# Layer 2 by kind of product in both layers' first slots, and w1's second half and w2 requested behind the gathered rows

## The chip, the cores and the metric

One of the eight cores of a Trainium2 chip runs the whole program. The metric is the device time of one execution in microseconds. TensorE does the matrix products, VectorE, ScalarE and GpSimd the elementwise work; SyncE (SP) mostly issues DMA requests, and GpSimd issues the indexed ones (gathers and scatters of rows).

## The reference, cut to what matters

An attention with a decaying state over 4 sequences of 768 tokens (8 heads of 64) gives 3072 rows of 512 numbers. Two mixture-of-experts layers follow, each with 8 experts; a row goes to one expert, the one with the largest logit:

```python
logits = x @ w_gate + modality_bias[modality_id]      # layer 1; layer 2 without the bias
e_idx = np.argmax(logits, axis=1)
for e in range(E):
    mask = e_idx == e
    h = np.maximum(x[mask] @ w1[e], 0.0)              # 512 -> 1024
    out[mask] = gate_w[mask, None] * (h @ w2[e])      # 1024 -> 512
```

Layer 2 skips rows whose `x @ w_skip` is not positive and adds its result to x.

## The kernel before, in words

**Precision.** Every product of the experts is done as three: each float32 factor is split into a high part (a cast to the matmul's format, `high`, `high_w2` on ScalarE) and a low part (the rest, a subtraction, `low`, `low_w2` on VectorE), and high x high, high x low and low x high are summed in PSUM. The tiles are `xth`/`xtl` (the rows, transposed), `w1h`/`w1l`, `hh`/`hl` (the hidden values after ReLU) and `w2h`/`w2l`; `raw1` and `raw2` hold the weights as loaded.

**Stages.** The attention runs over 24 units i (6 chunks of 128 tokens x 4 sequences). Each loads keys, queries and values, does its products, writes its row tile to `xs1` (`stage_x`), and each chunk's four tiles are routed: logits (`route_1`, copied to `lgt`), a transpose of them on TensorE and the bias (`route_2`), arg max and running sums `rs` on VectorE (`route_3`), the rank within the expert as two small products and the scatter of (row, gate) to a table `tab` (`route_4`, `route_5`). Then come the experts: the sorted rows are worked off in slots of 256 rows (two blocks of 128). A slot gathers its rows by the table (`load_ix`, `gather_x`), transposes them (`trans_x`), does `layer1` over eight blocks f of 128 hidden columns, two to a PSUM bank, and `layer2` over eight blocks c of the hidden dimension for either row block j. Layer 2 has the same slots over the rows of layer 1.

**The first slots.** `first1` begins before the last chunk is routed: its expert is chosen from earlier counts, its rows are gathered in unit 21, and in `layer1` the functions in `steps` and `mids` do the rest of the routing between the blocks f. The tables of later slots (`table`) are made on VectorE meanwhile, in three parts. `first2` is the same for layer 2. All others go through `slot`.

**Order.** Instructions run on each engine in the order in which the Python code issues them; semaphores are added where tiles depend on each other. SP's queue is in order too: a request that waits holds up all behind it. `behind(first, got)` makes a request wait for a gather's landing.

**Lines that the prediction uses** (numbers of the kernel before, which the profile has): L413 stores a row tile, L580 requests w1 by halves, L298 requests w2, L165 gathers; L304/L309 and L319/L322 split w1 and w2; L366 transposes gathered rows, L369/L370 cast them to `xth` and subtract to `xtl`; L548/L556 are attention products; L389 copies the logits to `lgt`, L392 transposes them; L133 are the running sums, L137/L138 the ranking products; L744 is layer 1's product, L751/L754 make `hh` and `hl`; L794, L795 and L796 are layer 2's three kinds of product, L806/L809 its result.

Of the kernel before, what the change touches and what calls it, by code (L numbers as in the profile page):

```python
# [35 lines left out]
def body(ctx: ExitStack, tc: tile.TileContext, qkv, cpk, w1, w2, wgr, out, dbg=None):  # L36
# [251 lines left out]
    def f32(ap):  # L288
        return ap.bitcast(F32)
# [12 lines left out]
    def high(n, cs):  # L302
        for c in cs:
            nc.scalar.copy(out=w1h[c][:, n * D:n * D + D], in_=raw1[:, c, n * D:n * D + D])  # L304
# [16 lines left out]
    def low_w2(c, eng=nc.vector):  # L321
        eng.tensor_tensor(out=w2l[c], in0=raw2[:, 2 * c:2 * c + 2], in1=f32(w2h[c]), op=ALU.subtract)  # L322
# [34 lines left out]
    def behind(first, got):  # L357
        for g in got:
            tc.add_manual_dep(first.ins, g.ins.name, mybir.DependencyInfo(mybir.DependencyClass.Sync, mybir.DependencyReason.DATA),
                              reason="the rows first")  # L360
# [59 lines left out]
    with ExitStack() as actx:  # L420
# [164 lines left out]
        for i in range(N):  # L585
# [13 lines left out]
            if i == N - 2:  # L599
                high(1, (0, 1))  # L600
# [7 lines left out]
            if i == 19:  # L608
                load_ix(0, 0, nc.sync.value_load(eb[0:1, 0, 1:2], min_val=0, max_val=E * TP - T))
                ld_w1_half(e0, 1)  # L610
            if i == N - 2:
                behind(ld_w2(e0), got0)
# [32 lines left out]
            if i == N - 2:  # L645
                low(1, (0, 1))
# [141 lines left out]
    def layer2(which, kk, j, hooks={}, cs=range(8)):  # L788
# [10 lines left out]
        if 7 not in cs:  # L799
            return  # L800
# [20 lines left out]
    def first1():  # L821
        tb = table(0)

        def last_x():
            high(1, (2, 3))
            low(1, (2, 3))
            stage_x(NC * B - 1, ptr[0])
            route_1()
            high_w2(0)
            low_w2(0, nc.gpsimd)  # L830
# [10 lines left out]
        def then():  # L841
            low_w2(1)
            next(tb)

        layer1(0, {0: last_x, 2: lambda: high_w2(1), 3: then, 5: lambda: split_w2([2]), 7: lambda: split_w2([3])},
               mids={1: mid, 3: late}, lead=True)
        next(tb)
# [10 lines left out]
        layer2(0, 0, 0)  # L858
        fl = flag(0, 1)
        layer2(0, 0, 1, {5: lambda: trans_x(0, 1, ptr), 6: lambda: split_next(0, 1, fl)})  # L860
        return fl, is_full(ei[0][0:1, 3 * KT + 1:3 * KT + 2])

    def first2():
# [3 lines left out]
        layer1(0, {0: la, 3: lambda: rb(pcnt[1]), 4: lambda: next(tb), 5: lambda: split_w2([1]),  # L867
               6: lambda: split_w2([2]), 7: lambda: split_w2([3])}, mids={1: rk}, lead=True)
# [11 lines left out]
        layer2(1, 0, 0)  # L880
        next(tb)
        fl = flag(1, 1)
        layer2(1, 0, 1, {5: lambda: trans_x(1, 1, ptr), 6: lambda: split_next(1, 1, fl)})

# [178 lines left out]
```

## Time and profile before

| | |
|---|---|
| median of 3 runs | 684.38 us (683.06 to 685.27) |
| the profiled execution | 685.24 us |
| its span | 683.3 us, of which matmuls in flight 659.0 us |
| granted TensorE clock | 0.996 of full speed |
| attention, to the first product of layer 1 | about 0 to 125 us |
| layer 1's first slot | 125 to 152 us |
| layer 2's first slot | 449.8 to 476 us |

A row of the timeline has the start, the length, the engine and line, the operation, what it writes and reads, and in brackets how long the engine stood idle before it and what released it. The ends of matmuls are modelled, and they overlap, so distances between starts tell more than lengths. Names of tiles stand without their numbers, so that `bank` is any PSUM bank and `xt` any row tile.

### The profile page before, as it was taken

To read this page: it belongs to the slowest core of one execution; us is meant where nothing else is said; L and a number is where in the kernel's file an instruction comes from. 1 tells how busy PE (TensorE), PEld (TensorE's weight loads), DVE (VectorE), ACT (ScalarE), POOL (GpSimd) and SP (SyncE) were. 2 spreads that over 40 slices of the span, in tenths; PEclk is the share of its full clock that TensorE was granted. 3 is DMA by queue.
4 is the path that set the end of the run, shared out by engine and by line. 5 is a ranking of instruction groups with operands and counts; after the bars stand their busy time and mean duration, and the time that the engine had idled before them with its cause. 6 is when DMAs were issued, how large, how long until landed. Compare 5 with 4: busy or idle time off the path is not lost. (4 is left out here: it accounts for less than half of the span.)

```text
span 683.3 us, 16287 instructions
## 1 busy us (share of the span) xinstructions
PE 659.0 (96%) x5388; PEld 587.0 (86%) x5388; DVE 437.0 (64%) x1147; ACT 258.2 (38%) x452; POOL 226.4 (33%) x288
## 2 busy tenths in 40 slices
PE   6999999899999999999999999999999999999993
PEld 5889988789988988889889988897998899888892
DVE  6656577684877916878778327868227575758650
ACT  2434435432122225832122227432225644566520
POOL 4356556461332331244322323323121112113321
PEclk9999999999999999999999999999999999999998
DMA  9768777739512232884211211633716658657500
GB/s 287 230 205 221 224 206 226 224 93 383 193 61 78 80 126 88 289 291 168 74 39 54 95 57 45 226 121 91 263 63 196 214 178 281 201 193 262 198 5 29
DMA packets 60653, 112.07 MB, mean 164 GB/s; under 512 B 18672, under 2 KB 18800, under 8 KB 60384
## 3 DMA queue, kind: packets, MB, share of 16 engines
q1 hardware_dynamic: 48544, 89.01, 39.7%
q0 software_dynamic: 9744, 20.47, 8.8%
q8 instruction: 62, 1.02, 0.7%
q10 hardware_dynamic: 2224, 0.93, 0.6%
q14 instruction: 79, 0.65, 0.3%
HBM read 86.44 MB, written 30.06 MB: 170 GB/s over the span
## 5 line engine op out<-in xcount | busy, mean ns | idle before, releaser
L744 PE MATMUL bank<-xth,w1h 128*128 128x256 f32 x672 | 188.4, 281 | 1.1 <-ACT xth L369 0.3
L744 PE MATMUL bank<-xth,w1l 128*128 128x256 f32 x672 | 187.0, 279 | 0.0
L744 PE MATMUL bank<-xtl,w1h 128*128 128x256 f32 x672 | 186.0, 278 | 0.1
L794 PE MATMUL bank<-w2h,hh 128*128 128x512 f32 x360 | 144.6, 402 | 0.0
L796 PE MATMUL bank<-w2h,hl 128*128 128x512 f32 x360 | 141.5, 393 | 0.3 <-DVE hl L776 0.3
L795 PE MATMUL bank<-w2l,hh 128*128 128x512 f32 x360 | 140.8, 391 | 0.9 <-DVE w2l L322 0.8
L744 PEld LDWEIGHTS bank<-xth,w1h 128*128 128x128 f32 x672 | 126.4, 188 | 3.4 <-issue 1.1
L744 PEld LDWEIGHTS bank<-xtl,w1h 128*128 128x128 f32 x672 | 126.1, 188 | 1.4 <-DVEq L816 0.4
L744 PEld LDWEIGHTS bank<-xth,w1l 128*128 128x128 f32 x672 | 126.4, 188 | 0.9 <-DVE w1l L316 0.7
L751 ACT ACTIVATE hh<-bank 128x512 fp32r<-128x512 f32 x84 | 50.3, 599 | 182.7 <-PE bank L744 141.8
L161 POOL DMA_INDIRECT out_dram<-x2r,it x43 | 51.2, 1190 | 191.6 <-DVE x2r L809 102.6
L754 DVE SCALAR_TENSOR_TENSOR hl<-bank,hh 128x512 fp32r<-128x512 f32 (+1 forms) x100 | 58.2, 601 | 84.2 <-ACT hh L751 78.4
L697 DVE CUSTOM_DVE_ANT_0 xtl<-x2r,wgb 128x512 fp32r<-128x512 f32 x108 | 74.3, 692 | 14.0 <-issue 8.7
L796 PEld LDWEIGHTS bank<-w2h,hl 128*128 128x128 f32 x360 | 67.6, 188 | 15.9 <-DVE hl L776 0.8
L795 PEld LDWEIGHTS bank<-w2l,hh 128*128 128x128 f32 x360 | 67.7, 188 | 15.7 <-DVE w2l L322 2.3
L161 POOL DMA_INDIRECT tab<-pk,rows x28 | 33.0, 1180 | 138.8 <-issue 92.1
L794 PEld LDWEIGHTS bank<-w2h,hh 128*128 128x128 f32 x360 | 67.7, 188 | 12.7
L165 POOL DMA_INDIRECT xg<-xs,it x54 | 58.4, 1081 | 27.7 <-issue 16.7
L322 DVE TENSOR_TENSOR w2l<-raw,w2h 128x1024 fp32r<-128x1024 f32 x47 | 54.7, 1219 | 4.4 <-ACT w2h L319 3.7
L319 ACT CAST w2h<-raw 128x1024 fp32r<-128x1024 f32 x48 | 49.3, 1050 | 20.4 <-issue 12.0
L806 ACT ACTIVATE x2r<-bank,it 128x512 f32<-128x512 f32 x26 | 17.9, 688 | 97.3 <-PE bank L796 76.8
L316 DVE TENSOR_TENSOR w1l<-raw,w1h 128x512 fp32r<-128x512 f32 x88 | 53.9, 684 | 0.6 <-ACT w1h L315 0.3
(207 smaller groups left out, 834.6 us busy)
## 6 DMA issues: line engine op xcount, KB each, us to landing
raw<-in_w_dram SPq DMA_DIRECT2D x96, 512.0 KB
kq<-in_qkv_dram SPq DMA_DIRECT2D x48, 256.0 KB
xs<-x2r SPq DMA_DIRECT2D x28, 256.0 KB
v<-in_qkv_dram SPq DMA_DIRECT2D x24, 256.0 KB
xs<-xr SPq DMA_DIRECT2D x24, 256.0 KB
xs<-xgm SPq DMA_DIRECT2D x7, 512.0 KB
wgb<-in_wgr_dram SPq DMA_DIRECT2D x1, 2304.0 KB
xg<-xs,it POOLq DMA_INDIRECT x54
```

The source lines that it names most:

```text
L161: nc.gpsimd.indirect_dma_start(out=dst, out_offset=bass.IndirectOffsetOnAxis(ap=idx, axis=0), in_=rows, in_offset=None, bounds_check=dst.s ...
L165: return nc.gpsimd.indirect_dma_start(out=rows, out_offset=None, in_=src, in_offset=bass.IndirectOffsetOnAxis(ap=idx, axis=0), bounds_chec ...
L316: nc.vector.tensor_tensor(out=w1l[c][:, s], in0=raw1[:, c, s], in1=f32(w1h[c][:, s]), op=ALU.subtract)
L319: nc.scalar.copy(out=w2h[c], in_=raw2[:, 2 * c:2 * c + 2])
L322: eng.tensor_tensor(out=w2l[c], in0=raw2[:, 2 * c:2 * c + 2], in1=f32(w2h[c]), op=ALU.subtract)
L697: nc.vector.tensor_tensor_reduce(out=xtl[kk % 2][:, :, j * P:(j + 1) * P], in0=x2r[kk % 2][j].rearrange("p (c t) -> p c t", t=P), in1=wgb[ ...
L744: nc.tensor.matmul(o, w[c][:, fs], x[:, c, :], start=(n == 0), stop=(n == 11))
L751: nc.scalar.activation(out=a, in_=pt, func=AF.Relu)
L754: nc.vector.scalar_tensor_tensor(out=b[:, q_], in0=pt[:, q_], scalar=0.0, in1=f32(a[:, q_]), op0=ALU.max, op1=ALU.subtract)
L794: nc.tensor.matmul(p2[j], a, w2h[g][:, i], start=(n == 0), stop=False)
L795: nc.tensor.matmul(p2[j], a, w2l[g][:, i], start=False, stop=False)
L796: nc.tensor.matmul(p2[j], b, w2h[g][:, i], start=False, stop=(n == 7))
```

## The change

Requests: w1's second half leaves unit 19, goes to unit 22 and waits for the first slot's gather (`behind`); w2 leaves unit 22 and goes to unit 23, without a wait of its own. Splits of w1's second half, two pieces of which were done in unit 22, are all done in `last_x`, behind the first block of layer 1. Splits of w2 in the first slots: the high parts are cast between the blocks of layer 1 as before, though at other places, and all low parts are subtracted behind layer 1, on VectorE, where one of four in `first1` was GpSimd's. Products of layer 2 in the first slots: `layer2_wide` does all high x high products of both row blocks, then low x high, then high x low, instead of the three kinds in turn for one block c after the other. The transposes of slot 1's rows follow 46 of the 48 products (before: 42). In `first2` the ranking products keep their place on TensorE, but the rest of the ranking goes ahead of the second ReLU; the last part of the table goes ahead of layer 2's products.

```diff
-    def low_w2(c, eng=nc.vector):
-        eng.tensor_tensor(out=w2l[c], in0=raw2[:, 2 * c:2 * c + 2], in1=f32(w2h[c]), op=ALU.subtract)
+    def low_w2(c):
+        nc.vector.tensor_tensor(out=w2l[c], in0=raw2[:, 2 * c:2 * c + 2], in1=f32(w2h[c]), op=ALU.subtract)
...
-            if i == N - 2:
-                high(1, (0, 1))
...
             if i == 19:
                 load_ix(0, 0, nc.sync.value_load(eb[0:1, 0, 1:2], min_val=0, max_val=E * TP - T))
-                ld_w1_half(e0, 1)
             if i == N - 2:
-                behind(ld_w2(e0), got0)
+                behind(ld_w1_half(e0, 1), got0)
+            if i == N - 1:
+                ld_w2(e0)
...
-            if i == N - 2:
-                low(1, (0, 1))
...
+    def layer2_wide(which, hooks):
+        n = 0
+        for kind in range(3):
+            for j in range(2):
+                js = slice(j * P, (j + 1) * P)
+                for c in range(8):
+                    x = (hh, hl, hh)[kind][c // 4][:, c % 4, js]
+                    w = (w2h, w2h, w2l)[kind][c // 2][:, c % 2]
+                    nc.tensor.matmul(p2[j], x, w, start=(kind == 0 and c == 0), stop=(kind == 2 and c == 7))
+                    if n in hooks:
+                        hooks[n]()
+                    n += 1
+                if kind == 2:
+                    finish(which, 0, j)
...
         def last_x():
-            high(1, (2, 3))
-            low(1, (2, 3))
+            high(1, range(4))
+            low(1, range(4))
             stage_x(NC * B - 1, ptr[0])
             route_1()
-            high_w2(0)
-            low_w2(0, nc.gpsimd)
...
         def then():
-            low_w2(1)
+            high_w2(1)
             next(tb)
-        layer1(0, {0: last_x, 2: lambda: high_w2(1), 3: then, 5: lambda: split_w2([2]), 7: lambda: split_w2([3])},
+        layer1(0, {0: last_x, 2: lambda: high_w2(0), 3: then, 5: lambda: high_w2(2), 6: lambda: high_w2(3)},
                mids={1: mid, 3: late}, lead=True)
+        for c in range(4):
+            low_w2(c)
...
-        layer2(0, 0, 0)
         fl = flag(0, 1)
-        layer2(0, 0, 1, {5: lambda: trans_x(0, 1, ptr), 6: lambda: split_next(0, 1, fl)})
+        layer2_wide(0, {45: lambda: trans_x(0, 1, ptr), 46: lambda: split_next(0, 1, fl)})
...
-        layer1(0, {0: la, 3: lambda: rb(pcnt[1]), 4: lambda: next(tb), 5: lambda: split_w2([1]),
-               6: lambda: split_w2([2]), 7: lambda: split_w2([3])}, mids={1: rk}, lead=True)
+        layer1(0, {0: la, 4: lambda: next(tb), 5: lambda: high_w2(1), 6: lambda: high_w2(2), 7: lambda: high_w2(3)},
+               mids={1: rk, 3: lambda: rb(pcnt[1])}, lead=True)
+        for c in range(1, 4):
+            low_w2(c)
...
-        layer2(1, 0, 0)
         next(tb)
         fl = flag(1, 1)
-        layer2(1, 0, 1, {5: lambda: trans_x(1, 1, ptr), 6: lambda: split_next(1, 1, fl)})
+        layer2_wide(1, {45: lambda: trans_x(1, 1, ptr), 46: lambda: split_next(1, 1, fl)})
```

SP's queue from the index load of the first slot on, before. `raw_136` is w1 as loaded, `raw_137` w2; `xr` are row tiles on their way to `xs`.

```order
L351 DMA it_158<-tab_61 128x2x4
L580 ISA
L580 DMA raw_136<-in_w_dram 128x2x512
...
L413 DMA xs_60<-xr_186 128x512
L438 DMA v<-in_qkv_dram 128x512
L413 DMA xs_60<-xr_187 128x512
L413 DMA xs_60<-xr_185 128x512
L298 ISA
L298 DMA raw_137<-in_w_dram 128x2x512
```

The same stretch now:

```order
L413 DMA xs_60<-xr_186 128x512
L438 DMA v<-in_qkv_dram 128x512
L413 DMA xs_60<-xr_187 128x512
L413 DMA xs_60<-xr_185 128x512
L580 ISA
L580 DMA raw_136<-in_w_dram 128x2x512
...
L413 DMA xs_60<-xr_186 128x512
L298 ISA
L298 DMA raw_137<-in_w_dram 128x2x512
```

w1's two requests (one is shown) stand behind three stores and the last load of values, and w2's four behind one more store.

ScalarE from the last but one row tile on, before. `w1h_138` to `w1h_141` are the four pieces of w1's high part, here of its second half; `xt_191` is the last unit's output.

```order
L304 CAST w1h_138<-raw_136 128x512
L304 CAST w1h_139<-raw_136 128x512
L412 COPY xr_186<-bank_199 128x512
L369 CAST xth_164<-bank_197 128x4x128
L369 CAST xth_164<-bank_200 128x4x128
L558 COPY xt_191<-bank_198 128x512
L304 CAST w1h_140<-raw_136 128x512
L304 CAST w1h_141<-raw_136 128x512
L412 COPY xr_187<-bank_196 128x512
L389 COPY lgt<-pmi 128x128
L319 CAST w2h_146<-raw_137 128x1024
```

And now:

```order
L412 COPY xr_186<-bank_199 128x512
L369 CAST xth_164<-bank_197 128x4x128
L369 CAST xth_164<-bank_200 128x4x128
L558 COPY xt_191<-bank_198 128x512
L304 CAST w1h_138<-raw_136 128x512
L304 CAST w1h_139<-raw_136 128x512
L304 CAST w1h_140<-raw_136 128x512
L304 CAST w1h_141<-raw_136 128x512
L412 COPY xr_187<-bank_196 128x512
L389 COPY lgt<-pmi 128x128
L748 ACTIVATE hh_1855<-bank_195 128x512
```

All four casts of w1's second half stand directly ahead of the copy of the last row tile and of `lgt`.

TensorE's second layer in the first slot of layer 1, before. `bank_200` and `bank_201` are the sums of the two row blocks; `w2h_146` to `w2h_149` and `w2l_150` to `w2l_153` the pieces of w2's high and low part.

```order
L794 MATMUL bank_200<-w2h_146,hh_1859 128x512
L795 MATMUL bank_200<-w2l_150,hh_1859 128x512
L796 MATMUL bank_200<-w2h_146,hl_1861 128x512
L794 MATMUL bank_200<-w2h_146,hh_1859 128x512
L795 MATMUL bank_200<-w2l_150,hh_1859 128x512
L796 MATMUL bank_200<-w2h_146,hl_1861 128x512
L794 MATMUL bank_200<-w2h_147,hh_1859 128x512
```

And now, its first group and the first rows of its last:

```order
L807 MATMUL bank_200<-w2h_146,hh_1855 128x512 x2
L807 MATMUL bank_200<-w2h_147,hh_1855 128x512 x2
L807 MATMUL bank_200<-w2h_148,hh_1856 128x512 x2
L807 MATMUL bank_200<-w2h_149,hh_1856 128x512 x2
L807 MATMUL bank_201<-w2h_146,hh_1855 128x512 x2
...
L807 MATMUL bank_200<-w2l_150,hh_1855 128x512 x2
L807 MATMUL bank_200<-w2l_151,hh_1855 128x512 x2
```

The first low part of w2 was read by the 2nd product and is now read by the 33rd; the last high part was read by the 19th and is now read by the 7th.

## Rows read from the trace of the kernel before

**Rows 1.** The page: busy time of the engines; one costly group.

```profile
PE 659.0 (96%) x5388; PEld 587.0 (86%) x5388; DVE 437.0 (64%) x1147; ACT 258.2 (38%) x452; POOL 226.4 (33%) x288
...
L322 DVE TENSOR_TENSOR w2l<-raw,w2h 128x1024 fp32r<-128x1024 f32 x47 | 54.7, 1219 | 4.4 <-ACT w2h L319 3.7
```

**Rows 2.** Timeline of TensorE where attention ends: start, length, operation, [idle before].

```profile
120.10 1.06 PE L548 MATMUL bank<-qs,sd 128*128 128x128 f32 x8
121.94 0.66 PE L366 MATMUL bank<-ident,xg 128*128 128x128 f32 x4 [0.78 <-DMA xg<-xs,it]
...
123.95 1.09 PE L556 MATMUL bank<-P,v 128*64 128x128 f32 x16
...
129.56 0.27 PE L392 MATMUL pmi<-ident,lgt 128*128 128x128 f32 x1
...
132.50 0.19 PE L137 MATMUL pmi<-oh,tri 128*128 128x32 bf16 x1
133.93 0.18 PE L138 MATMUL pmi<-rs,ones 128*128 128x32 bf16 x1 [1.24 <-DVE rs L133]
```

**Rows 3.** Timeline of TensorE, layer 2's products in layer 1's first slot.

```profile
139.88 0.40 PE L794 MATMUL bank<-w2h,hh 128*128 128x512 f32 x1
...
144.17 0.39 PE L794 MATMUL bank<-w2h,hh 128*128 128x512 f32 x1
144.64 0.50 PE L795 MATMUL bank<-w2l,hh 128*128 128x512 f32 x1
...
150.02 1.03 PE L366 MATMUL bank<-ident,xg 128*128 128x128 f32 x8
...
152.62 0.39 PE L744 MATMUL bank<-xtl,w1h 128*128 128x256 f32 x1
```

**Rows 4.** Timelines of VectorE and GpSimd: running sums, and a split of w2.

```profile
115.49 0.76 DVE L133 TENSOR_TENSOR rs<-rs,oh 128x8 bf16<-128x8 bf16 x4
...
131.21 2.86 DVE L133 TENSOR_TENSOR rs<-rs,oh 128x8 bf16<-128x8 bf16 x4
...
131.08 2.38 POOL L322 TENSOR_TENSOR w2l<-raw,w2h 128x1024 fp32r<-128x1024 f32 x1 [4.83 <-ACT w2h L319]
```

**Rows 5.** Timeline of GpSimd: second gathers of the first slot and of slot 1.

```profile
116.61 1.00 POOL L165 DMA_INDIRECT xg<-xs,it  x1 [0.31 <-issue]
...
146.68 1.15 POOL L165 DMA_INDIRECT xg<-xs,it  x1 [0.31 <-issue]
```

**Rows 6.** Timelines of SP's requests for weights and of ScalarE's first cast of w2.

```profile
103.02 1.00 SPq L580 DMA_DIRECT2D raw<-in_w_dram  x2
...
112.49 1.86 SPq L580 DMA_DIRECT2D raw<-in_w_dram  x2
...
123.47 5.22 SPq L298 DMA_DIRECT2D raw<-in_w_dram  x4
...
129.95 1.05 ACT L319 CAST w2h<-raw 128x1024 fp32r<-128x1024 f32 x1 [1.51 <-DMA raw<-in_w_dram]
```

**Rows 7.** Two stretches: length, engines' busy shares, clock, DMA share, GB/s (last).

```profile
103.00:107.60 4.60, 4.30 (x62) 3.51 (x64) 2.61 (x6) 2.28 (x5) 3.98 (x5) 1.00 0.78 233
...
112.50:118.40 5.90, 5.90 (x71) 5.19 (x70) 5.52 (x20) 2.91 (x6) 3.35 (x3) 1.00 0.63 173
```

**Rows 8.** Timeline of ScalarE: `lgt`, and the last ReLU of either first slot.

```profile
128.18 0.27 ACT L389 COPY lgt<-pmi 128x128 f32<-128x128 f32 x1 [0.41 <-PE pmi L387]
...
141.76 0.60 ACT L751 ACTIVATE hh<-bank 128x512 fp32r<-128x512 f32 x1 [2.97 <-remote]
...
462.64 0.60 ACT L751 ACTIVATE hh<-bank 128x512 fp32r<-128x512 f32 x1 [0.52 <-PE bank L744]
```

**Rows 9.** Timeline of TensorE, layer 2's products in layer 2's first slot.

```profile
462.20 0.40 PE L794 MATMUL bank<-w2h,hh 128*128 128x512 f32 x1
...
473.07 0.60 PE L366 MATMUL bank<-ident,xg 128*128 128x128 f32 x4
474.19 0.66 PE L366 MATMUL bank<-ident,xg 128*128 128x128 f32 x4 [0.52 <-DMA xg<-xs,it]
```

More of the change, by code (lines that the diff above doesn't have):

```diff
@@ L798, in layer2, with finish @@
                 hooks[n]()
-        if 7 not in cs:
-            return
+        if 7 in cs:
+            finish(which, kk, j)
+    def layer2_wide(which, hooks):
[12 more added lines that the diff above has]
+                    finish(which, 0, j)
+    def finish(which, kk, j):
         g = XG(which, kk)[j]
```

## The prediction

> **What bounds the kernel now.** I read the page's busy line first: TensorE has matmuls in flight for 659.0 of 683.3 us [rows 1]. So time can only come out of places where the matmul engine stands still, and the change touches two such places: the first slot of either layer. I then read TensorE's timeline over the first slot of layer 1 (120 to 153 us) and of layer 2 (450 to 476 us), and asked at each gap which engine or transfer ended it. What counts are distances between starts, since the listed ends are modelled.
>
> There are four gaps. (a) The last attention products start at 120.10 and the transposes of the first expert rows at 121.94, released by the gather's landing; the next attention products start at 123.95 [rows 2]. (b) The second ranking product starts 1.43 us after the first, 133.93 against 132.50, released by VectorE's running sums [rows 2]. There the sums need 2.86 us for four tiny additions that took 0.76 us one unit earlier, and the first of them starts 0.13 us after GpSimd began its split of w2's first low part (2.38 us) [rows 4]. (c) In the second layer's products one waits for w2's low part: 144.64 after 144.17, where the pace is (144.17 - 139.88)/18 = 0.238 us [rows 3]. (d) In layer 2's first slot the same wait costs more: 42 products lie between 462.20 and 473.07; at 0.234 us they need 9.83, so 1.04 us is waiting. The last four transposes there wait another 0.52 us for a gather [rows 9].
>
> **The change part by part.** All sums are made against the profiled execution, 685.24 us (683.3 of span, 1.9 around it). It is the slowest of the runs shown; the median is 684.38, and I subtract the difference from that.
>
> *The rows' gather first.* w1's second half (two requests, 1 MB) leaves the place behind unit 19 and now waits for the gather, with w2's four requests behind it. On SP's queue it moves past three stores and one load, which start earlier, and the gather no longer shares the DMA engines with it. The nearest undisturbed gather: the second one issued at 146.68 was in place when TensorE began its transposes at 150.02 without a wait [rows 3, 5], at most 3.34 us. The gather here was issued at 116.61 [rows 5], so its rows are there by 120.0, and TensorE reaches the transposes at 120.10 + 1.06 = 121.16. Gap (a) is 3.85 us between the rows, less 1.06 for the eight products before and 1.03 for eight transposes [rows 2, 3]: **1.76 us won**. Bounds: nothing (the gather is as late as now) to 1.76.
>
> *The price of asking late.* w1's second half is asked for at about 120.4. Its high parts are now all cast by ScalarE behind the first block of layer 1, ahead of the copy of the last row tile and of the logits' copy `lgt`, which TensorE needs for its transpose on L392. From the second request's landing T, ScalarE still has two casts (1.05 for as many elements), one 128x512 copy (0.6) and `lgt` (0.27) to do [rows 6, 8], with the steps between them 2.0 us. TensorE arrives at L392 at 129.56 - 1.76 = 127.8 [rows 2]. So every landing later than T = 125.8 is a new wait of the same length. How long does 1 MB of w1 take? The first half was asked for at 103.02, and by 107.60 the DMA engines had moved 4.6 us x 233 GB/s = 1.07 MB; the second half, asked for at 112.49, had its bytes by 118.40 (5.9 us x 173 GB/s = 1.02 MB) [rows 6, 7]. So T is 125.0 to 126.3. From the other side, w2's first half MB, asked for at 123.47, released ScalarE at 129.95, 6.5 us later [rows 6]; at that pace with another 1.4 us for the second request T is 128.3. The waits are 0, 0.5 and 2.5 us. I take **0.8 us lost**, near the two rows on w1 itself.
>
> The Trainium skill's page "DMA: Bandwidth & Descriptors" (section "Anatomy of one DMA — SWDGE (gpsimd) path") fits a transfer with about 2.0 us fixed and the bytes at 436 GB/s. By that (an estimate; it is fitted for GpSimd's queue) 1 MB lands 4.4 us after its request, at 124.8, and there is no wait at L392; by the rows above there is a small one. No run here shows so quick a load; the first rival says what it would give.
>
> *No split on GpSimd.* The four additions go back to 0.76 us and end before the first ranking product would: gap (b) goes, **1.40 us won** (its normal step is 0.03). VectorE's chain to the table (and the scatters, index loads and gather of slot 1) gets earlier by about the same.
>
> *Products by kind.* All 32 products with w2's high part come first, so the low parts are wanted 7.5 us after the start (32 x 0.234). Four splits follow each other on VectorE behind the last `hl`, 4 x 1.22 = 4.9 us [rows 1], and are in time. Gap (c): **0.3 us won**. But the high parts are wanted sooner: hh's last two blocks and w2h[3] by the 7th product, 1.4 us in, instead of the 19th. In layer 1 w2h[3] is cast ahead of hh's last block. That block's ReLU started 1.88 us after the first product (141.76 against 139.88), which nobody noticed; in layer 2 it started 0.44 us after (462.64 against 462.20) [rows 3, 8, 9]. With its 0.6 us it is ready at 2.48 or at 1.04; the first means a wait of 1.1. The same lateness would also push VectorE's last `hl`, the four splits and the rest of the table, which now stand in front of the low parts of slot 1's rows, by up to 1.5. Between 0 and 1.5 I take **0.6 us lost**.
>
> *The handover to slot 1.* The transposes of slot 1's rows came after 42 of 48 products and now come after 46: 4 x 0.23 = 0.92 us later. From their start to the slot's second product (the first that needs the low part of the rows) there are 2.60 us, 150.02 to 152.62 [rows 3]; that is a cast and a subtraction for either half, it does not shrink, and only two products are left to cover it instead of six. **0.92 us lost.**
>
> Layer 1's first slot: 1.76 + 1.40 + 0.3 - 0.8 - 0.6 - 0.92 = 1.14 us won.
>
> *Layer 2's first slot.* The 1.04 us of (d) goes. w2h[3] is cast after hh's last block: 462.64 + 0.6 + 1.05 = 464.3 [rows 6, 8], while the 7th product would start at 462.20 + 1.40 = 463.6: with the overlap of the two on ScalarE 0.6 lost. The transposes move back by 0.92: 473.07 - 1.04 + 0.6 + 0.92 = 473.55. The last four follow at 474.0 and find their rows, which were there at 474.19 before [rows 9] and whose table is ready sooner, as the ranking is now ahead of an `hl` on VectorE. From 474.19 to 474.0: 0.15 us won; -0.6 to +0.7 if the cast or the gather lies elsewhere.
>
> After these slots TensorE works on with the same instructions, and I find no later wait on the changed transfers, so the gain should last to the end. Sum: 1.14 + 0.15 = 1.3 us; 685.24 becomes 683.9, and the median 684.38 - 1.3 = **683.1**.
>
> **The rivals.** *No new wait*: w1's half lands before 125.8 and the last ReLU follows at once. Then 1.76 + 1.40 + 0.3 - 0.92 + 0.15 = 2.7 us, 681.7. For it: loads here meet an emptier queue than at 112.49, and layer 2's ReLU was prompt; against it: 5.9 and 6.5 us in the rows on loads. Chance 0.25. *Both prices in full*: the half lands at w2's pace (2.5) and the ReLU is late as in layer 1 now (1.5): 2.54 - 2.5 - 1.5 + 0.15 = 1.3 us slower, 685.7. For it: w2's load at nearly the same time, and the same place in the program; against it: both must come together. Chance 0.15. *The rows come no earlier*, the slower case of one mechanism: if the gather is held by stores or by its own latency, TensorE still gets its rows at 123.4, and now w1's half stands behind them: asked for at 123.47, it lands at 128.1 to 129.4, `lgt` follows 2.0 later and L392, at its old 129.56, waits 0.5 to 1.8, take 1.2. Then 1.40 + 0.3 - 1.2 - 0.6 - 0.92 + 0.15 = 0.9 us slower, 685.3. It decides from a landing of the gather after about 122: there (a) yields 0.9 less and the half comes 2 us later. For it: three stores still go ahead of the gather; against it: they are 0.75 MB, where 1 MB of w1 leaves. Chance 0.15.
>
> **How the numbers follow.** My forecast, with both prices at about the values taken, has 0.45, and its own range is 681.9 to 684.4. A measurement of this kernel tells about 0.3% (2.05 us) from no change. Faster by more: nearly all of the first rival (0.22) and a third of the forecast (0.14), 0.36. Slower by more: the tails of the last two, where the half is later still, and what I did not see, 0.12. The rest, 0.52, is within. The range goes from 1 us below the first rival to 0.3 above the second: 680.8 to 686.0.
>
> **What would show it.** The transposes on L366 at about 121.2 without a wait; one ranking product 0.03 to 0.05 after the other; TensorE waiting at L392 for ScalarE's `lgt` by 0.5 to 1; a wait of up to 1 at the 7th product of the first group; no wait at all for w2l; and slot 1's second product waiting about 1 us for `xtl` in both layers. I am wrong if the gather still lands at 122 or later, if w1's half needs more than 7 us, or if the splits on VectorE end after the 32nd product.

## The result, and the profile after

The changed kernel takes 688.50 us (median of 6 runs, 685.27 to 689.41), the kernel before on the same chip 683.94 (6 runs, 681.84 to 685.27): ratio 1.0065, interval 1.0043 to 1.0088, so 4.5 us slower (2.9 to 6.0). I had said 683.1, within 680.8 to 686.0. The profiled execution, 685.27 with a span of 683.4, is the fastest of the six, and one thing has to be known before its times are set against those of before: by attention unit 4, which the change doesn't touch, it is 2.0 us ahead (the unit's attention products start at 27.39 against 29.40), and the lead stays between 2.0 and 2.13 until unit 22. At unit 4 the profiles of this study lie between 2.2 us ahead of before's (e6) and 0.8 behind it (e5), and by unit 7 up to 1.4 behind (e1). So only distances are compared here.

TensorE's timeline of the changed kernel, where attention ends; the rows answer to [rows 2]. Line numbers shift from kernel to kernel: L807 is the product of `layer2_wide`, L741 (L747 in e6 and e12) layer 1's product, which is L744 of before, and L748 (L754 in e12) its ReLU; L235 to L284 make the table, L671 the zeros.

```profile
117.96 1.06 PE L548 MATMUL bank<-qs,sd 128*128 128x128 f32 x8
118.85 1.04 PE L366 MATMUL bank<-ident,xg 128*128 128x128 f32 x8
119.82 1.09 PE L556 MATMUL bank<-P,v 128*64 128x128 f32 x16
...
129.98 0.33 PE L392 MATMUL pmi<-ident,lgt 128*128 128x128 f32 x1 [4.46 <-ACT lgt L389]
134.50 0.19 PE L137 MATMUL pmi<-oh,tri 128*128 128x32 bf16 x1
134.54 0.18 PE L138 MATMUL pmi<-rs,ones 128*128 128x32 bf16 x1
```

Two gaps are gone as forecast: the transposes (L366) wait for nothing, and the ranking products are 0.04 us apart. In their place stands one of 4.46 us ahead of the logits' transpose. What released it is on ScalarE; first SP's requests, then ScalarE's timeline ([rows 6, 8] before).

```profile
118.70 1.03 SPq L580 DMA_DIRECT2D raw<-in_w_dram  x2
...
120.80 3.62 SPq L298 DMA_DIRECT2D raw<-in_w_dram  x4
```

```profile
125.24 1.14 ACT L304 CAST w1h<-raw 128x512 fp32r<-128x512 f32 x2 [3.70 <-DMA raw<-in_w_dram]
128.13 1.14 ACT L304 CAST w1h<-raw 128x512 fp32r<-128x512 f32 x2 [1.75 <-DMA raw<-in_w_dram]
129.18 0.58 ACT L412 COPY xr<-bank 128x512 f32<-128x512 f32 x1
129.66 0.27 ACT L389 COPY lgt<-pmi 128x128 f32<-128x128 f32 x1
```

w1's second half is asked for at 118.70 and ScalarE stands for it twice, to 128.13: 9.4 us after the request. From there to TensorE's transpose are 1.85 us, as forecast (2.0). Then comes what I had no term for. Stretches of the same profile, with the granted clock as third number from the right:

```profile
126.00:128.00 2.00, 0.00 (x0) 0.00 (x0) 1.19 (x2) 0.38 (x1) 0.00 (x0) 1.00 1.04 170
...
130.00:132.00 2.00, 2.00 (x13) 2.00 (x14) 1.49 (x9) 1.49 (x3) 0.00 (x0) 0.70 1.05 396
132.00:134.00 2.00, 2.00 (x11) 2.00 (x11) 1.07 (x4) 0.00 (x0) 0.00 (x0) 0.50 0.48 184
```

After the stand TensorE is busy again, but at a granted clock of 0.50 (1.2 instead of 2.4 GHz): 11 products in two microseconds, where the kernel before had up to 20. From L392 to L137 it needs 4.52 us instead of 2.94 [rows 2]. The kernel before was granted full speed from 12.5 us, where its record begins, to 678 us.

The handover to slot 1 on TensorE (answering to [rows 3]), and on VectorE:

```profile
140.32 3.90 PE L807 MATMUL bank<-w2h,hh 128*128 128x512 f32 x16
144.06 3.90 PE L807 MATMUL bank<-w2h,hl 128*128 128x512 f32 x16
147.79 3.43 PE L807 MATMUL bank<-w2l,hh 128*128 128x512 f32 x14
151.06 1.03 PE L366 MATMUL bank<-ident,xg 128*128 128x128 f32 x8
151.85 0.70 PE L807 MATMUL bank<-w2l,hh 128*128 128x512 f32 x2
153.53 0.38 PE L741 MATMUL bank<-xth,w1h 128*128 128x256 f32 x1 [0.97 <-DVE xtl L370]
154.15 0.38 PE L741 MATMUL bank<-xtl,w1h 128*128 128x256 f32 x1 [0.24 <-DVEq L830]
```

```profile
141.76 4.64 DVE L322 TENSOR_TENSOR w2l<-raw,w2h 128x1024 fp32r<-128x1024 f32 x4
146.33 0.35 DVE L235 TENSOR_TENSOR t_x<-t_h,eid 128x192 f32<-128x192 f32 x1
...
152.15 0.18 DVE L284 SCALAR_TENSOR_TENSOR ei<-t_r,t_w 128x22 int32<-128x22 f32 x1
152.81 1.29 DVE L370 TENSOR_TENSOR xtl<-bank,xth 128x512 fp32r<-128x512 f32 x2 [0.48 <-ACTq L830]
```

No product waits for a low part of w2. But VectorE now does four splits in a row (4.6 us), then the rest of the table (5.9 us to 152.3), and only then the low parts of slot 1's rows. In the kernel before the table ended at 150.3 and `xtl` then waited 0.95 us for ScalarE:

```profile
150.14 0.18 DVE L284 SCALAR_TENSOR_TENSOR ei<-t_r,t_w 128x22 int32<-128x22 f32 x1
151.27 1.29 DVE L370 TENSOR_TENSOR xtl<-bank,xth 128x512 fp32r<-128x512 f32 x2 [0.95 <-ACT xth L369]
```

All of it in one table, which also carries the experiments: distances in us between starts on TensorE, worked out from each run's timeline. The stations are the last attention unit's first products (L548 of before), its attention products (L556), the logits' transpose (L392), the ranking (L137), layer 2's first product, slot 1's second product and slot 2's first. e10, which changes only the second expert layer, is left out; its sum, with the code of before up to there, is 56.6, so two profiles of the same code can differ by 0.7.

| kernel | to L556 | to L392 | to L137 | to layer 2 | to slot 1's 2nd | to slot 2 | sum | median, before beside it |
|---|---|---|---|---|---|---|---|---|
| before | 3.85 | 5.61 | 2.94 | 7.38 | 12.73 | 24.79 | 57.3 | 684.38 |
| changed | 1.86 | 10.16 | 4.52 | 5.83 | 13.83 | 24.78 | 61.0 | 688.50, 683.94 |
| changed, again (e9) | 2.08 | 9.38 | 2.94 | 5.82 | 14.86 | 26.40 | 61.5 | 690.5 (one run), 684.33 |
| e1 early half | 3.57 | 5.53 | 2.94 | 5.82 | 13.80 | 24.73 | 56.4 | 684.63, 684.23 |
| e2 late half alone | 1.86 | 9.59 | 4.52 | 5.84 | 12.67 | 24.78 | 59.3 | 687.19, 684.23 |
| e3 logits first | 1.86 | 5.55 | 2.94 | 7.14 | 15.36 | 26.13 | 59.0 | 685.14, 684.23 |
| e4 rows early | 1.86 | 9.57 | 4.53 | 5.61 | 14.90 | 24.73 | 61.2 | 687.04, 684.23 |
| e5 e3 + zeros on ScalarE | 1.86 | 5.61 | 2.94 | 7.29 | 13.67 | 24.72 | 56.1 | 684.24, 684.14 |
| e6 both halves first | 2.17 | 5.60 | 2.94 | 5.82 | 13.38 | 24.72 | 54.6 | 682.94, 684.14 |
| e7 w2 later | 1.86 | 9.19 | 4.53 | 5.63 | 15.14 | 26.06 | 62.4 | 689.68, 684.14 |
| e8 split on VectorE | 3.61 | 5.61 | 2.94 | 5.82 | 13.36 | 24.74 | 56.1 | 683.35, 684.14 |
| e11 stand filled | 1.86 | 10.91 | 2.85 | 5.62 | 15.17 | 24.72 | 61.1 | 691.27, 684.33 |
| e12 rows sooner | 2.59 | 6.07 | 2.94 | 5.82 | 14.69 | 25.14 | 57.3 | 687.17, 684.33 |

(In e9 the stretch at half clock lies ahead of the logits, at 126 to 130 us, and so within the second distance.) For the changed kernel's first profile: 2.0 won at the rows, 4.55 lost for the logits, 1.58 lost to the clock, 1.55 won at the ranking, 1.1 lost at the handover: 3.7 us slower, against 4.5 between the medians. (The two profiled executions took 685.24 and 685.27: the changed one was 2.1 us ahead where the table begins, and spent 1.5 us less behind it.)

Five of the profiles (before, e9, e10, e11, e12) share something that no edit put there. Of some 50 operations of ScalarE that wait for TensorE alone, one or two start more than 1 us after the modelled end of their product, the last ReLU of layer 1's first slot in each; in the nine others none does. The trace has the signals too: at that ReLU ScalarE starts 0.02 to 0.03 us behind TensorE's signal in all fourteen, so the signal is late, not ScalarE. In the same five about a fifth of the records of landings is missing. e9 to e12 ran on one chip, e1 to e8 on two others, and the changed kernel has it in one of its two profiles (e9). So it goes with the execution and not with the kernel; why is open. A difference between one of these five and another profile can come from it.

### The profile page after: what moved, and what is told of

It reads as the page before. It is cut to its first block, busy times and chain, and to the rows that moved or that the text cites. A ratio compares the mean times of both kernels' runs of the same rounds, so it can differ in the third digit from the quotient of the medians.

```text
span 683.4 us, 16284 instructions
## 1 busy us (share of the span) xinstructions
PE 657.1 (96%) x5388; PEld 586.4 (86%) x5388; DVE 435.6 (64%) x1148; ACT 257.8 (38%) x452; POOL 224.2 (33%) x287
## 5 line engine op out<-in xcount | busy, mean ns | idle before, releaser
L741 PE MATMUL bank<-xth,w1h 128*128 128x256 f32 x672 | 189.1, 282 | 2.0 <-DVE xtl L370 1.0
L741 PE MATMUL bank<-xth,w1l 128*128 128x256 f32 x672 | 187.4, 279 | 0.0
L741 PE MATMUL bank<-xtl,w1h 128*128 128x256 f32 x672 | 186.5, 279 | 0.7 <-DVEq L830 0.7
L791 PE MATMUL bank<-w2h,hh 128*128 128x512 f32 x328 | 132.0, 402 | 0.0
L741 PEld LDWEIGHTS bank<-xth,w1h 128*128 128x128 f32 x672 | 127.2, 189 | 5.0 <-ACTq L830 2.2
L793 PE MATMUL bank<-w2h,hl 128*128 128x512 f32 x328 | 128.7, 392 | 0.3 <-DVE hl L773 0.3
L741 PEld LDWEIGHTS bank<-xtl,w1h 128*128 128x128 f32 x672 | 126.7, 189 | 1.9 <-DVEq L830 1.0
L792 PE MATMUL bank<-w2l,hh 128*128 128x512 f32 x328 | 127.9, 390 | 0.0
L741 PEld LDWEIGHTS bank<-xth,w1l 128*128 128x128 f32 x672 | 127.2, 189 | 0.4 <-DVE w1l L316 0.4
L748 ACT ACTIVATE hh<-bank 128x512 fp32r<-128x512 f32 x84 | 50.3, 599 | 180.3 <-PE bank L741 166.7
L793 PEld LDWEIGHTS bank<-w2h,hl 128*128 128x128 f32 x328 | 61.6, 188 | 14.9 <-DVE hl L773 0.7
L792 PEld LDWEIGHTS bank<-w2l,hh 128*128 128x128 f32 x328 | 61.7, 188 | 12.2
L791 PEld LDWEIGHTS bank<-w2h,hh 128*128 128x128 f32 x328 | 61.7, 188 | 11.5
```

The lines of the kernel that those rows point to most:

```text
L741: nc.tensor.matmul(o, w[c][:, fs], x[:, c, :], start=(n == 0), stop=(n == 11))
L748: nc.scalar.activation(out=a, in_=pt, func=AF.Relu)
L791: nc.tensor.matmul(p2[j], a, w2h[g][:, i], start=(n == 0), stop=False)
L792: nc.tensor.matmul(p2[j], a, w2l[g][:, i], start=False, stop=False)
L793: nc.tensor.matmul(p2[j], b, w2h[g][:, i], start=False, stop=(n == 7))
```

## The experiments

**e1 and e2: the late request without the rest of the change, and the rest without it.** e2 is the kernel before with the late requests and, with them, the splits of w1's second half in `last_x`; e1 is the changed kernel without both.

```diff
+                ld_w1_half(e0, 1)                        # e1, at unit 19
-                behind(ld_w1_half(e0, 1), got0)          # unit 22
-                ld_w2(e0)                                # unit 23
+                behind(ld_w2(e0), got0)                  # unit 22
```

> The changed kernel, with w1's second half asked for and cast where the kernel before has it; w2 stands behind the rows, and the products by kind, the splits on VectorE and the later transposes stay. Theory A (asking late is the price: TensorE stands 4.5 us for the logits behind the casts, and then works 3.4 us at half clock, about 1.4 us more): both go, the win of the rows' early landing (2.0) goes as well, the sums' win (1.4) and layer 2's win (about 1.4) stay and the handover costs 1.1 to 1.4: 682 to 683.5, with no half clock in the middle. Rival B (the products by kind and the handover behind them are the price): it stays at 687 or more.

> The kernel before with one part of the change alone: w1's second half is asked for behind the rows' gather, w2 behind it, and the four high and low parts of that half are made behind the first block of layer 1; the split on GpSimd and the products by group stay. Theory A: the wait for the logits appears here too (4.5 us, then a stretch at half clock, 1.4), less the 2.0 won at the rows: 687 to 688.5, slower than before by 3.5 to 4.5. Rival B: within 1 us of before.

Measured: e1 684.63 against 684.23, ratio 1.0002 (0.9988 to 1.0016); e2 687.19, ratio 1.0045 (1.0030 to 1.0059). The stand and the half clock are in e2 and not in e1. e2's TensorE, and a stretch of it:

```profile
130.69 0.33 PE L392 MATMUL pmi<-ident,lgt 128*128 128x128 f32 x1 [3.88 <-ACT lgt L389]
```

```profile
132.00:134.00 2.00, 2.00 (x11) 2.00 (x10) 1.93 (x3) 1.69 (x4) 1.79 (x1) 0.50 0.99 383
```

So the late request, with its casts ahead of `lgt`, carries the loss, 3.0 of the 4.5 us in e2: theory A holds for the cause, though e2 was to be 3.5 to 4.5 slower than before. Theory A was too kind to the rest: e1 was to be 0.7 to 2.2 us faster than before and is not. Its distances show the ranking's win (1.56) and a handover 1.07 longer. e2 shows that win too (5.84), though it keeps the split on GpSimd and its running sums take 2.83 us: at half clock TensorE came to the ranking no sooner than the sums were done.

**e3: the logits ahead of the casts.**

```diff
-            high(1, range(4)); low(1, range(4))
             stage_x(NC * B - 1, ptr[0]); route_1()
+        def casts(): high(1, range(4)); low(1, range(4))    # steps[1]: behind the second block
```

> The changed kernel; only the four casts and splits of w1's second half move on ScalarE and VectorE behind the last row tile's copy, the logits' copy and the last ranking (to behind the second block of layer 1). Theory A: TensorE finds its logits, no stand of 4.5 us at the logits' transpose, no half clock behind it; what the load's lateness still costs appears at the fifth block, which needs that half: four casts of 0.5 after a landing at about 128 end at 130.5, near where TensorE would come, with the low parts after them: 0 to 2 us of waiting. 681.5 to 684. Rival (the casts are not what holds the logits, TensorE would wait at that place for something else): 687 or more. Rival C (the wait only moves to the fifth block in full): 686 to 688.

685.14, ratio to before 1.0017 (1.0003 to 1.0031): some 3.4 us of the 4.5 are back, though the time is 1.1 above theory A's range. The distance to L392 is 5.55, there is no half clock at 131, and the late half costs 1.3 at the fifth block (to layer 2: 7.14 instead of 5.82), so what held TensorE were casts that it did not need yet. But the handover became 15.36, with a half-clock stretch behind it (26.13). The rows: e3's VectorE, e3's GpSimd, then VectorE of e5 below.

```profile
149.10 1.61 DVE L283 TENSOR_SCALAR t_w<-t_w 128x22 f32<-128x22 f32 x1
150.74 0.18 DVE L284 SCALAR_TENSOR_TENSOR ei<-t_r,t_w 128x22 int32<-128x22 f32 x1
151.39 1.29 DVE L370 TENSOR_TENSOR xtl<-bank,xth 128x512 fp32r<-128x512 f32 x2 [0.47 <-DVE ei L284]
```

```profile
149.23 0.51 POOL L671 MEMSET x2r<- 128x512 f32 x1
149.69 0.98 POOL L671 MEMSET xgm<- 128x512 f32 x2
```

```profile
150.09 0.18 DVE L283 TENSOR_SCALAR t_w<-t_w 128x22 f32<-128x22 f32 x1
```

A VectorE operation of 0.18 us takes 1.61 while GpSimd clears three tiles, and ends with it (150.71 against 150.67). The Trainium skill's page "SBUF — State Buffer" (section "SBUF: two separate sides") says that the two engines share a pair of ports, which some of VectorE's operations need, and that whichever starts first keeps it for its whole instruction while the other stops; these rows agree, over three of GpSimd's instructions in a row.

**e5: e3 with GpSimd's zeros written by ScalarE.**

```diff
-        for t in (x2r[1][1], xgm[0], xgm[1]):
-            nc.gpsimd.memset(t, 0.0)
+        for t in (x2r[1][1], xgm[0], xgm[1]):
+            nc.scalar.activation(out=t, in_=bc(ones[:, 0:1], [P, D]), func=AF.Copy, scale=0.0)
...                                                  # wgp likewise
```

> The kernel e3_logits_first with one more edit: the zeros and the gate copy that GpSimd writes behind the gathers (five small writes to wgp, x2r and xgm) are made by ScalarE, which stands still there. Theory D (the handover's 2.4 us in e3 are partly GpSimd's writes holding up VectorE: the table's operation at that moment took 1.61 us, where the same took 0.18 in the kernel before): 1.4 us less at slot 1's second product, and with a shorter stand the half clock behind it may go as well (up to 1.3): 682.5 to 684. Rival (the low parts wait for the rows or for the table anyway): 685.

684.24, ratio 0.9999 (0.9988 to 1.0011): 0.9 less than e3, a little above the range expected. The handover went from 15.36 to 13.67 and the half clock behind it is gone: theory D.

**e7: is it w2 that makes w1's half late?**

```diff
-            if i == N - 1:
-                ld_w2(e0)
             stage_x(NC * B - 1, ptr[0])
+            ld_w2(e0)
```

> The changed kernel; only w2's four requests move from 2.1 us behind w1's second half to behind the last row tile's store, so that the half is on the queue without them. If w2 shares the engines and makes the half late, it lands 2 to 3 us earlier, the stand at the logits' transpose is 1.5 to 2.5 us instead of 4.5: 685.5 to 687, with w2's high parts still in time. Rival (the load is slow by itself, its first packets taking up to 2 us): the stand stays at 4 us or more, 688 to 689.

689.68, ratio 1.0068 (1.0054 to 1.0082). SP and ScalarE of e7:

```profile
121.44 1.03 SPq L580 DMA_DIRECT2D raw<-in_w_dram  x2
...
132.13 2.12 SPq L298 DMA_DIRECT2D raw<-in_w_dram  x4
```

```profile
128.46 1.14 ACT L304 CAST w1h<-raw 128x512 fp32r<-128x512 f32 x2 [4.14 <-DMA raw<-in_w_dram]
129.93 1.14 ACT L304 CAST w1h<-raw 128x512 fp32r<-128x512 f32 x2 [0.33 <-DMA raw<-in_w_dram]
```

With w2 asked for 2.2 us after the half was already in use, the half still needs 8.5 us; the stand is 3.48, between the two answers, and the time is above both, with a handover of 15.14 and a second stretch at half clock behind it (26.06). The 8.5 us lie inside the spread of the profiles with w2 alongside (7.7 to 9.8), so no share of w2 is shown and the load is slow by itself. Nor is it this place alone: w1's first half, asked for in unit 18, needed 6.6 to 8.6 us in the fourteen profiles. The trace shows where the changed kernel's 9.4 us went. In the first 3.75 us the DMA engines moved 57 GB/s, in the next 3.75 us 385. And the semaphore that tells of a transfer's landing rises in sixteen steps: fifteen of the second request's had come by 125.18, the last at 128.11, where the cast starts. In the other late profiles the last step lags the fifteenth by 0.1 (e9) to 2.6 us (e4), in e7 by 1.4. What holds up the start and the last step stays open.

**e8: the split on VectorE alone**, the kernel before with w2's first low part made by VectorE, behind the fourth block.

```diff
-            low_w2(0, nc.gpsimd)                     # last_x
+            low_w2(0)                                # then
             low_w2(1)
```

> The kernel before; only w2's first low part is made by VectorE, ahead of its second, behind the fourth block, instead of by GpSimd. By the prediction's step on that split, the running sums need 0.8 instead of 2.9 us and the second ranking product follows the first at once: 1.4 us faster, 682.5 to 683.3, if VectorE's 1.2 us more do not delay the low parts of slot 1's rows. Rival (they come back at the handover, as VectorE's row of table and splits is what the rows' low parts wait for): 684 to 684.5.

683.35, ratio 0.9983 (0.9969 to 0.9998). To layer 2 it needs 5.82 instead of 7.38, 1.56 less, and at the handover 0.63 more: the measured 0.8 us, between the two theories.

**e10: layer 2's part alone**, the kernel before with the changed `first2`.

```diff
-        layer2(1, 0, 0)
-        layer2(1, 0, 1, {5: lambda: trans_x(1, 1, ptr), 6: lambda: split_next(1, 1, fl)})
+        layer2_wide(1, {45: lambda: trans_x(1, 1, ptr), 46: lambda: split_next(1, 1, fl)})
```

> The kernel before, with the change in layer 2's first slot alone (products by kind, high parts by ScalarE, low parts last, ranking's second half behind the fourth block, transposes behind the 46th product). The prediction gives it 0.15 us (684.0); the distances of the traces give 0.5 to 1.2 (683.0 to 683.6).

684.05 against 684.33, ratio 0.9993 (0.9979 to 1.0008): 0.3 us, which does not contradict the forecast of 0.15.

**e9: the changed kernel again.**

> The changed kernel once more, for a second profile: the one at hand (685.27) is the fastest of its six runs, the others lie 2 to 4 us above it at a mean granted clock of 0.990 to 0.991 instead of 0.993. If these 2 to 4 us are the handover, a stand of 1 us there has become 2.4 us, as in e3 and e7, with a second stretch of 3.41 us at half clock behind it. If they are the logits, the stand at the logits' transpose is 6 us or more. If it comes out near 685 again, this stays open.

690.5 us, one run without an interval. Its TensorE up to the logits and at the handover, its last ReLU on ScalarE, and a stretch behind them:

```profile
126.64 0.58 PE L741 MATMUL bank<-xth,w1h 128*128 128x256 f32 x1 [1.70 <-ACT xth L369]
...
132.64 0.27 PE L392 MATMUL pmi<-ident,lgt 128*128 128x128 f32 x1
...
141.40 1.56 PE L807 MATMUL bank<-w2h,hh 128*128 128x512 f32 x6
143.52 2.57 PE L807 MATMUL bank<-w2h,hh 128*128 128x512 f32 x10 [0.56 <-ACT hh L748]
...
155.63 0.38 PE L741 MATMUL bank<-xth,w1h 128*128 128x256 f32 x1 [1.32 <-DVE xtl L370]
```

```profile
142.87 0.60 ACT L748 ACTIVATE hh<-bank 128x512 fp32r<-128x512 f32 x1 [1.62 <-PE bank L741]
```

```profile
158.00:160.00 2.00, 2.00 (x12) 2.00 (x11) 0.00 (x0) 0.00 (x0) 0.00 (x0) 0.50 0.91 332
```

No answer holds as it was put. Of the 5.2 us between the two profiles of the changed kernel, 3.2 lie ahead of the last attention unit, 0.5 in the table's stations and 1.5 behind them. Within the stations the losses lie elsewhere than in the first profile. TensorE stood 1.70 us at layer 1's first block for `xth`, as the signal of the transposes came late, and worked at half clock from 126.4 to 129.8. ScalarE again stood for w1's half, until 130.15, but `lgt` was there at 131.94 and TensorE came to L392 only at 132.64, so no stand for the logits shows.

The handover was the first answer, and it holds in part: it lost 2.1 instead of 1.1, with a stand of 1.32 and not 2.4, and a second stretch at half clock cost 1.6 (26.40 against 24.79). It begins with the last ReLU, again behind a late signal: it starts 1.47 us after layer 2's first product, where in the first profile it started 0.20 after, and pushes the last `hl`, the four splits, the table and `xtl`. In the kernel before it started 1.88 after [rows 3, 8], but there the 19th product was the first to read that block, 4.29 after. The mean granted clock of the other five runs of the changed kernel (0.990 to 0.991, against 0.993 in its profile) fits two stretches in these too, but they have no trace, and what makes them 2 to 4 us slower stays open.

**e11: the stand filled** with 19 products that nobody reads, ahead of the logits' transpose.

```diff
+            for _ in range(19):
+                nc.tensor.matmul(p2[1], xth[0][:, 0, 0:P], w1h[0][:, 0:D], start=True, stop=True)
             route_2(NC - 1)
```

> The changed kernel with 19 products of 128x512 on TensorE ahead of the logits' transpose, into a bank that nobody reads then: 4.4 us of work in the place of the stand. Theory E (the half clock behind the stand comes from the stand, and costs 1.4 us of its own): no stretch at half clock at 131 us, and 0.8 to 1.6 us faster than the changed kernel, though TensorE does more: 686.5 to 687.7. Rival (the stretch belongs to the place or to the load, not to the stand): it stays, 688 to 689.

In the slot theory E holds: no stretch at half clock, and L392 to L137 takes 2.85 instead of 4.52.

```profile
130.00:132.00 2.00, 2.00 (x11) 1.60 (x10) 1.00 (x2) 1.66 (x4) 0.00 (x0) 1.00 1.02 327
132.00:134.00 2.00, 2.00 (x12) 1.64 (x11) 0.36 (x2) 1.57 (x3) 0.00 (x0) 1.00 1.06 407
```

The time did not follow: 691.27, ratio 1.0115 (1.0095 to 1.0135). The added products ended later than the logits came (10.91), the handover was a long one (15.17), and behind the slot there are waits of another 3 us that the other profiles don't have. As a test of the sum it is a miss. It is one of the five profiles with late signals (its last ReLU starts 1.77 after layer 2's first product), and on its chip the changed kernel's one run took 690.5.

**e4 and e12: the transposes sooner.** e4 changes the changed kernel, in both layers; e12 changes e6, in layer 1.

```diff
-        layer2_wide(0, {45: lambda: trans_x(0, 1, ptr), 46: lambda: split_next(0, 1, fl)})
+        layer2_wide(0, {41: lambda: trans_x(0, 1, ptr), 44: lambda: split_next(0, 1, fl)})   # e4
+        layer2_wide(0, {43: lambda: trans_x(0, 1, ptr), 45: lambda: split_next(0, 1, fl)})   # e12
```

> The changed kernel; only the transposes of slot 1's rows and the next split go back to where they stood, behind the 42nd and the 45th product instead of the 46th and 47th, in both layers. By the prediction's price of the handover (0.92 in layer 1, about the same in layer 2, where the rows themselves may be late) it is 0.9 to 1.8 us faster than the changed kernel: 686.5 to 687.5. By the profile's larger price of layer 1's handover (1.1 to 1.4) 1.5 to 2.5 faster. If the low parts of the rows wait for VectorE's table anyway, no difference: 688.

> The kernel e6_both_halves_first with slot 1's transposes two products sooner in layer 1 (behind the 44th product, the next split behind the 46th). There TensorE waits 0.52 and 0.24 us for the rows' parts; if the transposes set that, 0.4 us less (682.5); if VectorE's table and splits set it, which end 0.5 us ahead of the rows' low parts, or the rows' landing, nothing (682.9).

e4: 687.04, ratio to before 1.0046 (1.0031 to 1.0061), 1.5 us below the changed kernel's median and in the range that the prediction's price gave, though the two intervals overlap. In layer 1 nothing was won at the handover, which is 14.90 in its profile: the rows land late (0.53 us of waiting) and the low parts wait for VectorE in any case. In the second expert layer the price holds: from the first slot's first layer 2 product to slot 1's second product it needs 12.89 us, the changed kernel 13.72, 0.83 less. e12: 687.17, ratio 1.0047 (1.0028 to 1.0065), 4 us slower than e6, against both answers. In its profile two operations of ScalarE begin late:

```profile
125.47 0.59 ACT L558 COPY xt<-bank 128x512 f32<-128x512 f32 x1 [1.66 <-PE bank L556]
...
139.46 0.60 ACT L754 ACTIVATE hh<-bank 128x512 fp32r<-128x512 f32 x1 [1.64 <-PE bank L747]
```

The first starts 2.35 us after the attention products that it copies, in e6 1.14 (121.82 after 120.68). The second is again the last ReLU, 1.50 us after layer 2's first product, in e6 0.20, and the handover is 14.69. Both lie ahead of the products whose order e12 changes, and both follow a late signal of TensorE. e6 ran on another chip and has none, so the 4 us are not shown to come from the edit.

**e6: a version that is faster than both on the chip where it ran.** e1, with w1's second half asked for right behind the first, in unit 18, and the zeros on ScalarE.

```diff
                 ld_w1_half(e0, 0)
+                ld_w1_half(e0, 1)
```

> The kernel e1_early_half with w1's second half asked for right behind the first (behind unit 18), so that neither stands ahead of the rows' gather nor behind it, and the same zeros on ScalarE as in e5. If asking late is the whole price of the early rows, this has the rows' gain (2.0) without a wait for the logits, and the handover's 0 to 1.4: 681 to 683. Rival (another MB ahead of the attention's loads makes these late, or the gather is no earlier): 684 to 686.

682.94 against 684.14, ratio 0.9984 (0.9971 to 0.9996), in the range of the first answer. Its TensorE:

```profile
119.41 1.34 PE L366 MATMUL bank<-ident,xg 128*128 128x128 f32 x8
126.28 0.27 PE L392 MATMUL pmi<-ident,lgt 128*128 128x128 f32 x1
...
147.81 0.38 PE L747 MATMUL bank<-xth,w1h 128*128 128x256 f32 x1 [0.52 <-ACTq L836]
148.43 0.39 PE L747 MATMUL bank<-xtl,w1h 128*128 128x256 f32 x1 [0.24 <-DVEq L836]
```

The rows come early (2.17), the logits do not wait, no clock is lost: 2.7 us in the slot, of which 1.2 show in the median. e12, nearly the same kernel, was slower than before on another chip.

## Why the prediction was wrong

**The step that failed is the price of asking late.** I took 0.8 us, with 2.5 as the worst; it cost 4.55, and 1.58 more through the clock. The mechanism and its place were right (ScalarE's casts ahead of `lgt`, 2.0 us from the landing to L392; measured 1.85), and so was the condition that I named for being wrong: w1's half needs more than 7 us. What was mis-sized is the landing. My 4.6 and 5.9 us came from stretches in which the DMA engines moved about 1 MB [rows 7]. That is a sum of bytes over all transfers; no row there shows anyone receiving w1. The same trace has the landings: the last recorded steps of the two halves' semaphores came at 109.62 and 119.16, 6.6 and at least 6.7 us after their requests. By these the wait would have been 1.3 us or more, and the rest is what the load took longer behind the gather. The only landing in my rows was w2's, 6.5 us for half of it [rows 6], and it would have given 7.9. From the request to the second pair of casts, where ScalarE waited for the transfer, it took 7.7 us (e9) to 9.8 (e5) in the eight profiles with the late request. The sentence on the Trainium skill's page "DMA: Bandwidth & Descriptors" (section "Anatomy of one DMA — SWDGE (gpsimd) path"), which is fitted for GpSimd's queue, would have had 4.4 by my estimate; the trace doesn't agree.

**A term was missing: the clock.** The kernel before lost it nowhere between 12.5 and 678 us, so no row of it gave a price. The slow stretch follows the stand and not the late load: in e3 and e5 the load is as late, TensorE finds its logits, and there is none at 131; in e11 the stand is filled, and there is none either.

**The rows' gather first** was right: 1.8 (e9) to 2.0 won, forecast 1.76, in every kernel with that order. **No split on GpSimd** was right in its place (1.39 between the two ranking products, forecast 1.40), but e8 shows that 0.6 of it comes back where VectorE is the bound, and e2 that behind the late request the gap was gone with the split as well. **The handover and the products by kind** together were forecast at 1.22 lost (0.92 + 0.6 - 0.3) and measured 1.1 in the first profile and 2.1 in the second. That the first is so near is partly luck: the ReLU was prompt there (0.20), so the 0.6 for it was not lost, and the way from the transposes to slot 1's second product, which I held fixed at 2.60, took 3.09. I named the late ReLU and the splits ahead of `xtl`, and counted neither GpSimd's zeros nor the clock behind a long handover; the 1.88 us that I took for the ReLU belong to the executions with late signals, as e8, with the same casts, has 0.20. **Layer 2** was right within what can be measured: from the first slot's first layer 2 product to slot 1's second product the changed kernel needs 13.72 us, before 14.10, and e2 and e8, which leave this slot alone, 13.66 and 14.08.

The rival *Both prices in full* was nearest in mechanism, though only its late landing came true in the first profile, and stopped at 685.7 because its price was w2's pace without the clock.

## What to carry to other kernels

Read how long a load takes from an engine that waited for it or from the last step of its semaphore, not from a stretch's bytes; where no engine ever waited for that load, put the bound well above the other landings. When a request moves later, look at what stands in program order behind the first use of its data: here a copy of 0.27 us that needed none of it held TensorE for 4.5 us, and moving it ahead of the casts gave back 3.4. And where a change makes a busy TensorE stand for some microseconds, count that twice, once for the wait and once for the slower clock that may follow it.

## What the runs showed of the hardware

- After stands of 3.5 to 4.5 us at the logits (changed, e2, e4, e7), after handovers with a stand of 2.4 us (e3, e7), and in e9 after a stand of 1.70 for `xth` and a handover of 1.32, TensorE worked at a granted clock of 0.50 for some microseconds; such a stretch cost 1.3 to 1.6 us, where the table tells it apart from the wait. After handovers with stands of 0.5 to 1.35 us (changed, e1, e4, e5, e6, e11, e12) it did not.
- Clearing writes of GpSimd held up a 0.18 us operation of VectorE to 1.61 us (e3), and to 0.48 where they met for less (the changed kernel has 0.48 for L283).
- 1 MB of weights took 7.7 to 9.8 us from request to use here, alone in the queue (8.5) or not, and the last of the sixteen steps of its semaphore came up to 2.9 us behind the fifteenth. Asked for in unit 18 it took 6.6 to 8.6 us to the last step.
- In five executions (before, e9, e10, e11, e12) TensorE's signal at the last ReLU of layer 1's first slot came 1.3 to 1.7 us after the modelled end of the product, and ScalarE started within 0.03 us of it; in the nine others the signal came within 0.02 us of that end. Why stays open.
